# A fused RWKV-7 recurrence and expert mixture: a reciprocal and a block turn moved in VectorE's stated order, and five more filler products on TensorE

## The chip, the cores and the metric

The kernel runs on one core of a Trainium2 chip. The metric is the time of one execution on the device in microseconds (us), median of several runs. Before the change it is 1106.38 us, the median of three runs between 1105.45 and 1107.4. One further execution was taken by the profiler: it lasted 1112.95 us, and 1110.9 us of it lie between its first and its last instruction.

## The reference, cut to what matters

The inputs r, k, v, w, a, b have the shape (4, 8, 768, 40): batch, heads, tokens, width of a head. The first part walks along the tokens with a state of 40x40 for each head; the second part is a mixture of four experts with ReLU, weighted by normalized probabilities, over the 3072 rows of 320 that the first part gives.

```python
for t in range(S):
    y[:, :, t] = np.einsum('bhd,bhde->bhe', rt, state)
    Sa = np.einsum('bhde,bhe->bhd', state, at)
    state_decay = state * wt[:, :, None, :] - np.einsum('bhd,bhe->bhde', Sa, bt)
    state = state_decay + np.einsum('bhd,bhe->bhde', vt, kt)
...
x = np.ascontiguousarray(attn_out.transpose(0, 2, 1, 3)).reshape(B * S, H * D)
for e in range(E):
    h = np.maximum(x @ w1[e], 0.0)
    out += p[:, e:e + 1] * (h @ w2[e])
```

## The kernel before, in words

**Units.** The recurrence is computed in chunks of 64 tokens. A unit is one chunk for two of the four batches, with all eight heads, so that the 128 partitions hold 2 x 64 tokens (or, turned, two heads of 64 channels). There are 12 chunks and 24 units, numbered `u` = 0 to 23; units 2c and 2c+1 belong to chunk c. Names such as `M15` or `AT16` in VectorE's order mean the instruction of that kind for that unit.

**What happens for one unit.** `within` (L501) turns the decays and takes their running product (`G`, `scan`, L566), takes the reciprocal of it (`1/gp`, L582 for units from 8 on, where the decays lie by channel), turns and scales a into `AT` (L624, L626), and b and k into `NT` and `KT` (L638 to L644: the turn of k, then its product with `gp`). TensorE multiplies these into the 64x64 matrix `F` of each head (`pfe`, L663), which ScalarE copies out (L669). `substitute` (L716) inverts the unit triangular matrices of `F`: VectorE copies two parts of `blocks` (L721) and ScalarE two, VectorE turns them into `M` (L733), clears the diagonal (`M0`, L739), and folds every second column into the first by the two operations `Z1` (L745) and `Z2` (L749, whose output is `M` again). Then GpSimd runs 16 steps of one product (L763) and two sums (L780) on `Z`. `merge` (L786) turns the result on VectorE (`Qc` L791, `QTc` L792), and TensorE completes the inverse by the products `pY` and `pQ`. `step` (L824) applies the inverse to the state (`prn`, `psat`, `pxr`, `pdy`), adds up outputs and state on VectorE, and sends the output rows by DMA into `xT`, the input of the mixture.

**The mixture** of a chunk (`mixture_of_chunk`, L1070) fills TensorE's time between those products. For each expert and each half of its hidden units, `up_last` and `up_main` compute `ph` (in two PSUM buffers), ScalarE makes `hs` of it with ReLU (L976), and VectorE forms five sums of `hs` for an expert (`sum_a`, L1102: tiles a1, a7, a5, a2, a6, numbered through the kernel). The second products `p431`, `p75`, `p26` are scaled by a gate and added into `osb` on VectorE (L991), one or two operations with `gate` and one with `minus_gate` for each product. `ph` and these products share three PSUM buffers in turn (the tag `mm`).

**What sets the order.** The main loop (L1309 to L1429) calls the generators of several units piece by piece: in the turn of `u` it runs the step of `u`, the substitution of `u + 2` on GpSimd, and the loads of `u + 3`. TensorE's instructions keep this order (`stated`, L104). VectorE's order is left to a scheduler, which goes by the order of the calls and their priority, and is bound by pairs "this one ahead of that one" (L1433 to L1442): the list `VECTOR_ORDER` for the early units and lists of pairs for the later ones, among them `ahead_of_merge`. An engine runs its instructions strictly in the order of the built program, and waits where an input is not there. SyncE (SP) issues nearly all DMAs, also in order. The tile `gp` has one buffer, `rawA` (the loaded a) too; `AT` has two.

**The start.** In the first 45 us unit 0 is computed alone, and there VectorE runs the 16 steps of the substitution itself (L763, L774). TensorE has little to do; `keep_warm(n)` (L1209) gives it n products of the identity with itself, whose result nobody reads. Each counts as two matmuls in the profile. One group of ten stands at L1252, directly before `pY` of unit 0.

Of the kernel before, what the change touches and what calls it, by code (L numbers as in the profile page):

```python
# [33 lines left out]
def kernel(  # L34
# [48 lines left out]
    NU = NC * B // 2  # L83
# [25 lines left out]
    def matmul(**k):  # L109
        return stated(nc.tensor.matmul(**k))  # L110
# [101 lines left out]
    BY_CHANNEL = 8  # L212
# [53 lines left out]
    def load(q, names):  # L266
        for x in names:
            if x == "V":
                t = sb.tile([P, H, D], FP32, name="natV", tag="natV", bufs=2)[:]
            else:  # L270
                t = by_tokens(x, q.u)
            q.n[x] = t
            for i, bb in enumerate(q.b):
                nc.sync.dma_start(
                    out=t[i * L:(i + 1) * L], in_=srcs[x][bb, :, q.c * L:(q.c + 1) * L, :].rearrange("h t e -> t h e"),
                )
# [914 lines left out]
    def run(gen, n=99):  # L1191
        if gen is None:
            return
        for _ in range(n):
            if next(gen, gen) is gen:
                break
# [12 lines left out]
    def keep_warm(n):  # L1209

        for _ in range(n):
            ins = matmul(out=warm[:, 0:P], lhsT=ident[:], rhs=ident[:], start=True, stop=True)
            tc.keep_in_program_order(ins)
# [35 lines left out]
    keep_warm(8)  # L1249
    run(norm, 1)  # L1250
    run(ws[1], 1)
    keep_warm(10)  # L1252
    load(units[2], "W")
    for x in "VR":
        load_padded(units[2], x)
# [181 lines left out]
    ahead_of_merge = [(f"QTc{u - 1}", f"{x}r{u}.{i}") for u in range(BY_CHANNEL, NU) for x in "BK" for i in range(2)]  # L1437
    ahead_of_merge += [(f"QTc{u - 1}", f"RH{u - 1}.{r}") for u in range(BY_CHANNEL, NU) for r in range(2)]
    ahead_of_merge += [(f"QTc{u - 1}", f"VC{u}.{r}") for u in range(BY_CHANNEL, NU) for r in range(2)]
    in_second = [("Zr1.14", "out0"), ("out0", "Zm1.16")]  # L1440
    for one, then in [*zip(names, names[1:]), *((f"out{n}", x) for n, x in moved), ("blocks0.3", "VCv1"), ("blocks0.3", "ETc0.0"), ("blocks1.3", "Zu1.0"), ("blocks1.3", "Zu1.3"), *turned_ahead, *in_second, *waits_of_scalar, *ahead_of_merge]:
        tc.add_manual_dep(made[then].ins, made[one].ins.name, BEHIND, reason="stated order of VectorE")  # L1442
# [30 lines left out]
```

## Time and profile before

| | us |
|---|---|
| median of three runs | 1106.38 |
| the profiled execution | 1112.95 |
| its span, first to last instruction | 1110.9 |
| TensorE (PE) busy | 1071.4 (96%) |
| VectorE (DVE) busy | 808.5 (73%) |
| GpSimd (POOL) busy | 538.7 (48%) |
| ScalarE (ACT) busy | 343.9 (31%) |
| mean granted clock of TensorE | 0.977 |

A line of the timeline gives the start of an instruction (or of several alike) from the span's start, its duration, the engine, the line of the kernel, the operation with its output and inputs, and in square brackets how long the engine had been idle before it and what released it. A line of the view by stretches gives for each stretch the busy time of each engine with its count of instructions, then the clock granted to TensorE (1.00 is full speed), the share of the DMA engines that was busy and the traffic. A line of the view of waits has who waited, for whom, and then the sum of the waits in us, how many, and the longest.

### The profile page before, as it was taken

The numbers are of one execution on the slowest core, as the hardware profiler recorded it, in microseconds if no ns is written. First come the engines' busy times: TensorE is split into PE (matmuls) and PEld (weight loads), VectorE is DVE, ScalarE is ACT, GpSimd is POOL, SyncE is SP. The second block draws the span as 40 slices with busy tenths as digits, with TensorE's granted clock in tenths as the row PEclk, the third lists the DMA queues.
The fourth block names the chain that finished last, engine by engine and source line by source line (L and its number), as shares of the span: only waits on it lengthen the run. The fifth ranks groups of instructions, "written<-read, shape, count | busy, mean of one in ns | idle before, by whom it ended". The sixth has DMA issues, their size and how long they took to land.

```text
span 1110.9 us, 38458 instructions
## 1 busy us (share of the span) xinstructions
PE 1071.4 (96%) x16012; PEld 960.2 (86%) x16012; DVE 808.5 (73%) x1565; ACT 343.9 (31%) x942; POOL 538.7 (48%) x1322
## 2 busy tenths in 40 slices
PE   7899999999999999999999899899899989999998
PEld 7778888888989889899889889898898988998887
DVE  7786779996886977877959678686785967553443
ACT  3433444332322323323333323233232332321110
POOL 6116777746447356457355463553635546430000
PEclk9899999999999999999999899899999989999999
DMA  6775643435444444543453542443444343031230
GB/s 119 192 200 127 136 105 108 102 80 108 118 88 107 109 93 96 114 103 91 108 116 85 111 98 62 113 119 61 102 111 94 85 109 91 25 92 56 62 94 12
DMA packets 275349, 111.04 MB, mean 100 GB/s; under 512 B 229816, under 2 KB 254952, under 8 KB 275176
## 3 DMA queue, kind: packets, MB, share of 16 engines
q1 hardware_dynamic: 271192, 107.75, 42.1%
q8 instruction: 126, 2.06, 0.8%
q10 hardware_dynamic: 3984, 0.84, 0.4%
q14 instruction: 47, 0.39, 0.1%
HBM read 100.65 MB, written 3.93 MB: 94 GB/s over the span
## 4 chain that ended last, share of the span: by engine, by line
PE 47%; POOL 22%; DVE 17%; issue 7%; SPq 4%; DMA 2%; ACT 1%; ACTq 0%; DVEq 0%; POOLq 0%
PE ph L110 20%; PE p L110 16%; POOL Z L780 14%; POOL Z L763 8%; DVE M L733 3%; DVE a L1102 3%; SPq L936 2%; DVE osb L991 2%; SPq L302 2%; PE po L110 2%; PE pdy L110 1%; PE prn L110 1%; DVE blocks L721 1%; DVE Z L745 1%; DVE M L749 1%
## 5 line engine op out<-in xcount | busy, mean ns | idle before, releaser
L780 POOL TENSOR_TENSOR Z<-Z 128x31 f32<-128x31 f32 (+7 forms) x704 | 258.1, 367 | 55.1
L110 PE MATMUL ph<-xT,w1b 128*128 128x256 f32 (+3 forms) x1536 | 228.3, 387 | 0.5 <-issue 0.5
L110 PE MATMUL ph<-xT,w1a 128*128 128x256 f32 (+3 forms) x1536 | 225.8, 385 | 0.0
L1102 DVE TENSOR_TENSOR a<-hs 128x512 f32<-128x512 f32 x220 | 156.1, 728 | 91.5 <-ACT hs L976 91.5
L976 ACT ACTIVATE hs<-ph 128x512 f32<-128x512 f32 (+1 forms) x208 | 116.6, 565 | 311.4 <-PE ph L110 308.8
L763 POOL TENSOR_TENSOR Z<-M,Z 128x62 f32<-128x62 f32 (+7 forms) x352 | 148.0, 421 | 107.0 <-DVE M L749 81.2
L110 PEld LDWEIGHTS ph<-xT,w1b 128*128 128x128 f32 (+1 forms) x1536 | 172.5, 166 | 28.4 <-issue 7.0
L110 PEld LDWEIGHTS ph<-xT,w1a 128*128 128x128 f32 (+1 forms) x1536 | 171.1, 165 | 28.8 <-issue 7.7
L110 PE MATMUL p<-sums,a 128*128 128x160 f32 x1056 | 164.9, 299 | 0.0
L991 DVE SCALAR_TENSOR_TENSOR osb<-p,gate,osb 128x320 f32<-128x320 f32 (+1 forms) x243 | 107.6, 481 | 65.9 <-PE p L110 62.7
L110 PEld LDWEIGHTS p<-sums,a 128*128 128x128 f32 x1056 | 152.8, 190 | 2.2
L726 POOL COPY below<-F 32x256 f32<-32x256 f32 x48 | 29.3, 611 | 218.3 <-ACT F L669 153.6
L110 PEld LDWEIGHTS p<-w,hs 128*128 128x128 f32 x704 | 98.6, 190 | 9.0 <-issue 7.8
L110 PE MATMUL p<-w,hs 128*128 128x160 f32 x704 | 104.9, 302 | 0.4 <-DVE osb L991 0.4
L110 PE MATMUL p<-w,a 128*128 128x160 f32 x704 | 102.8, 299 | 0.0
L110 PEld LDWEIGHTS p<-w,a 128*128 128x128 f32 x704 | 98.0, 190 | 0.0
L798 POOL COPY QT<-QTc 32x256 f32<-32x256 f32 x96 | 44.1, 460 | 60.7 <-DVE QTc L792 54.4
L896 ACT COPY RS<-pxr 64x256 f32<-64x256 f32 x88 | 32.4, 368 | 115.6 <-DVE SX L499 80.9
L791 DVE STREAM_TRANSPOSE Qc<-Z 128x256 f32<-128x256 f32 x24 | 14.9, 621 | 57.6 <-POOL Z L780 57.4
L582 DVE RECIPROCAL gp<-G 128x512 f32<-128x512 f32 x16 | 53.6, 3352 | 0.5
L733 DVE STREAM_TRANSPOSE M<-blocks 128x1024 f32<-128x1024 f32 x24 | 47.0, 1958 | 1.7 <-ACT blocks L721 0.6
L707 ACT COPY EV<-pev 64x160 f32<-64x160 f32 x96 | 23.1, 288 | 80.1 <-PE pev L110 79.8
(167 smaller groups left out, 1458.6 us busy)
## 6 DMA issues: line engine op xcount, KB each, us to landing
w1a<-in_moe_w_dram SPq DMA_DIRECT2D x37, 512.0 KB
w1b<-in_moe_w_dram SPq DMA_DIRECT2D x37, 512.0 KB
w<-in_moe_w_dram SPq DMA_DIRECT2D x4, 1280.0 KB
w1a<-in_moe_w_dram SPq DMA_DIRECT2D x74, 64.0 KB
w1b<-in_moe_w_dram SPq DMA_DIRECT2D x74, 64.0 KB
out_dram<-osb SPq DMA_DIRECT2D x45, 80.0 KB
rawW<-in_w_dram SPq DMA_DIRECT2D x48, 72.0 KB
natV<-in_v_dram SPq DMA_DIRECT2D x42, 80.0 KB
```

The source lines that it names most:

```text
L110: return stated(nc.tensor.matmul(**k))
L582: pin(noted(nc.vector.reciprocal(out=gp[:], in_=G[:, :, 1:L + 1]), "1/gp", q.u))
L707: nc.scalar.copy(out=of_slot(q.EV[half(p)], i ^ p)[:, :, 0:D], in_=pev[i][half(p)])
L726: tc.keep_in_program_order(nc.gpsimd.tensor_copy(out=q.below[quarter(i)], in_=q.F[quarter(i), :, 0:Q]))
L733: ins = nc.vector.transpose(out=M[:], in_=cols)
L763: ins = eng.tensor_tensor(out=Z[:, 1:3, 0:n, j + 1:Q], in0=M[:, j:j + 2, None, j + 1:Q].to_broadcast([P, 2, n, m]), in1=Z[:, here, 0:n, j: ...
L780: eng.tensor_tensor(out=z[:, 0], in0=z[:, 0], in1=z[:, x], op=ALU.add)
L798: ins = nc.gpsimd.tensor_copy(out=q.QT[quarter(i), :, quarter(i % 2)], in_=QTc[quarter(i)])
L896: nc.scalar.copy(out=RS[half(s), x ^ s::2], in_=prs[x][half(s)].rearrange("p (j i) t -> p j i t", i=2),)
L976: ins = nc.scalar.activation(out=h[:, i * HF // 2:(i + 1) * HF // 2, 0:n], in_=ph[i][:], func=ACTF.Relu,)
L991: ins = nc.vector.scalar_tensor_tensor(out=to, in0=p, scalar=sc, in1=to, op0=ALU.mult, op1=ALU.add)
L1102: ins = nc.vector.tensor_tensor(out=t[:], in0=x, in1=y, op=op)
```

## The change

The call before the first `pY` gets 15 instead of ten fillers, and two lists of pairs join the stated order of VectorE. The first asks that the reciprocal of unit u+2 go ahead of five A sums of the mixture; the second that `M` of unit u go ahead of the turn of `AT` of unit u+1.

```diff
@@ -1249,7 +1249,7 @@
     keep_warm(8)
     run(norm, 1)
     run(ws[1], 1)
-    keep_warm(10)
+    keep_warm(15)
     load(units[2], "W")
@@ -1437,6 +1437,8 @@
     ahead_of_merge += [(f"QTc{u - 1}", f"VC{u}.{r}") for u in range(BY_CHANNEL, NU) for r in range(2)]
+    ahead_of_merge += [(f"1/gp{u + 2}", f"sum_a{10 * u - 45 + n}") for u in range(BY_CHANNEL, NU - 2) for n in range(5)]
+    ahead_of_merge += [(f"M{u}", f"AT{u + 1}") for u in range(BY_CHANNEL, NU - 1)]
     in_second = [("Zr1.14", "out0"), ("out0", "Zm1.16")]
```

Set side by side, the two built programs differ in these places and no others. On TensorE five fillers more stand before the first `pY`. On VectorE the turn of `AT` and its product with `G` move in three places (units 9, 10 and 11), and the reciprocal in four (units 16, 18, 20 and 22); in the other places of the two lists the stated order held already. On SP one piece of `rawA` (32x8x48 elements) of the start is issued in front of four pieces of weights instead of behind them. The orders of VectorE, before on the left:

```
AT (units 9 and 10, from the AT turn on)   | 1/gp (units 16, 18, 20, 22), from the scan on
before              after                  | before                      after
turn AT             gate, sum_a, minus     | scan                        scan
gate, sum_a, minus  blocks (2)             | a1, KT turn (2)             KT turn (2), KT x gp
blocks (2)          M                      | a7, KT x gp                 1/gp
AT x G              turn AT                | gate p75, a5, minus p75     gate p75, gate p26
M, M0               M0, AT x G             | gate p26, a2, minus p26     minus p75, minus p26
Z1, Z2              Z1, Z2                 | a6                          a1, a7, a5, a2, a6
                                           | blocks (2), 1/gp, M         blocks (2), M
```

For unit 11 the turn of `AT` stood before far ahead of `M10`, between the two operations on `NT`, and its product with `G` behind the scan; after the change both stand between `M10` and `Z1` as in the other two places.

## The prediction

> **What bounds the kernel now.** The page first: PE is busy for 96% of the span. That is an average, so the next view is the one of waits: what does TensorE still wait for?
>
> ```profile
> PEld pY L110 <- issue: 24.5, 17, 2.9
> PE pY L110 <- DVE QTc L792: 24.2, 14, 2.8
> ```
>
> Nearly all of its waiting stands before one product, `pY`, and ends with the turn `QTc` of VectorE. The timeline of PE tells where:
>
> ```profile
> 12.02 0.63 PE L113 MATMUL pNT<-ident,n_tok 128*128 128x128 f32 x4 [1.32 <-DVE n_tok L618]
> ...
> 31.80 0.68 PE L110 MATMUL pY<-QTc,below 64*64 64x64 f32 x16 [2.38 <-DVE QTc L792]
> ...
> 318.86 0.59 PE L110 MATMUL pY<-QTc,below 64*64 64x64 f32 x13 [1.04 <-DVE QTc L792]
> ...
> 574.27 0.59 PE L110 MATMUL pY<-QTc,below 64*64 64x64 f32 x13 [1.53 <-DVE QTc L792]
> ...
> 620.48 0.98 PE L110 MATMUL pY<-QTc,below 64*64 64x64 f32 x13 [2.82 <-DVE QTc L792]
> ```
>
> From 574 on the gaps alternate: 1.52 to 1.53 at 574, 667, 759, 851 and 943, and 2.78 to 2.82 at 620, 713, 805 and 897 (call them the short and the long gaps). A gap costs more than itself, as the view by stretches shows around the two (PEclk is the third number from the right):
>
> ```profile
> 574.00:576.00 2.00, 1.73 (x82) 1.76 (x86) 0.79 (x3) 0.96 (x4) 1.58 (x4) 0.82 0.17 49
> 576.00:578.00 2.00, 2.00 (x30) 1.69 (x26) 1.65 (x6) 0.71 (x3) 0.00 (x0) 0.50 0.15 31
> 578.00:580.00 2.00, 2.00 (x22) 1.75 (x20) 1.96 (x3) 1.03 (x4) 0.00 (x0) 0.82 0.61 117
> ```
>
> The short gap is followed by half speed for (0.18 + 0.50 + 0.18) x 2 / 0.5 = 3.4 us, the long one by 6.8 (same sum over 618 to 628). The gaps of 1.32 and 1.04 in the timeline above are not: their stretches read 1.00. In work: from the start of `pY` to the start of the `p` product behind the next 128-row `ph` it takes 6.43 us at 276, where the gap is 0.30 (282.46 - 276.03), 8.05 at 574 (582.32), 9.36 at 620 (629.84). So a short gap costs 1.53 + 1.62, a long one 2.82 + 2.93.
>
> What makes a long gap long? VectorE ahead of it:
>
> ```profile
> 578.73 1.23 DVE L566 TENSOR_TENSOR_SCAN G<-G,first 128x520 f32<-128x520 f32 x1
> 583.15 0.69 DVE L1102 TENSOR_TENSOR a<-hs 128x512 f32<-128x512 f32 x1 [3.19 <-ACT hs L976]
> 583.76 0.77 DVE L324 STREAM_TRANSPOSE KT<-rawK 128x256 f32<-128x256 f32 x2
> ...
> 589.08 1.43 DVE L721 COPY blocks<-F 32x256 f32<-32x256 f32 x2
> 590.54 3.35 DVE L582 RECIPROCAL gp<-G 128x512 f32<-128x512 f32 x1
> 593.81 1.88 DVE L733 STREAM_TRANSPOSE M<-blocks 128x1024 f32<-128x1024 f32 x1
> ...
> 619.24 0.61 DVE L791 STREAM_TRANSPOSE Qc<-Z 128x256 f32<-128x256 f32 x1 [4.46 <-POOL Z L780]
> ```
>
> `blocks` is done, and `M` waits behind a reciprocal that only unit 16 needs, a turn later. From `M` the chain of waits goes without slack through `Z1`, `Z2`, GpSimd's 16 steps, `Qc` and `QTc` to `pY`. And VectorE stood idle 3.19 us earlier, behind the scan that the reciprocal reads.
>
> **The reciprocal (four places, each before a long gap).** New order: the scan ends at 579.96; the two turns of k (0.69), its product (0.60), the reciprocal (3.30): 584.6. `KT` needs `rawK`, whose four DMAs SP issues from 565.07 to 567.65, 12.3 us ahead; in the turn before 367.85 they were issued until 357.74, and `KT` ran 10.1 us later without waiting, so I expect no wait. `p75` is ready about then (PE runs its 16 passes from 582.32, done about 584.65): first gate 0.46, 585.1. The second gate waits for `p26`, done on PE about 586.9, and now all five A sums stand behind it. Then: gate 0.46, two minus 0.30 each, five sums 0.61 each, `blocks` 1.45, together 5.6: `M` at 592.5 instead of 593.81. Of the 3.3 us that the reciprocal takes out, 1.3 reach `M`; the rest becomes idle time before the second gate. Bounds: if nothing were lost there, 2.8 (the whole gap); if `KT` waited for `rawK` until 583.7, -0.6.
>
> A side cost: the next `ph` (587.28) takes the PSUM buffer of `p75`, free after its minus: 587.06 before, about 587.7 now. PE stands about 0.45 us there, but the remaining gap at `pY` covers it: 2.82 - 1.3 = 1.5 splits into 0.45 there and 1.05 before `pY`. Without that cover it would cost 4 x 0.45 = 1.8 in all. The sums' readers are late enough: `a1` is read about 595, made by 589.
>
> The clock: a gap of 1.05, or even 1.3, is of the kind that no half speed followed. So a long gap loses 1.3 + 2.93 = 4.2 us, four of them 16.9. What is late next is the short gap; its `M` is paced by the gates behind PE's products (632.05 and 634.23 both wait for PE) and moves along with PE, so its 1.52 stay. Its half speed may not: today the turns repeat every 92.2 us, and every short gap is punished alike; half speed comes in portions of 3.4 us, and 92.2 is 27 of them. With a turn of about 88 the gaps drift against these portions, and one that straddles a border has less than 1.32 us on either side. I count one of the five, 1.6; bounds 0 and 8.1.
>
> Here the Trainium skill speaks against the gain. "TensorE: Matmul & The Clock Gate", section "Why this matters for your kernels", asks only that gaps stay under about 3 us. By it neither the gap of 2.82 nor that of 2.38 would be punished, and the sum would be 4 x 1.3 = 5.2. The rows above have half speed after 1.53 us, and I go by them.
>
> **`M` ahead of the turn of `AT` (three places).** The turn (0.63) and its product with `G` (0.61) leave the place before `M`, but come back between `M` and `Z1`; GpSimd's first step waits for `Z2`:
>
> ```profile
> POOL Z L763 <- DVE M L749: 81.2, 22, 6.0
> ```
>
> For units 9 and 10 the sum up to `Z2` is the same: 0, at most -0.1 each for the 0.08 us between `M` and `M0` that the turn now fills. For unit 11 both come from far ahead (363.50 and 367.24). That costs nothing only while VectorE is dense from there to `M10` at 379.09, and it stays so: the gates would start 1.24 earlier, at 371.4 and 373.9, with `p75` and `p26` done on PE about 371.0 and 373.3. If they waited all the same: up to 1.24, which makes a gap of 1.02 into 2.3, with its half speed up to 4 us. I take 0. `rawA` is free later; SP's next loads into it stand at 318.88, 338.87 and 382.74, the turns will end about 295.3, 338.4 and 380.7: no wait.
>
> **Five fillers.** Ten take 2.40 us at 27.02, so five take 1.2, inside the gap of 2.38 before `pY` of unit 0, which waits for `QTc` (31.30, VectorE's own substitution, untouched). The gap becomes 1.18, below 1.32. Half speed from 32.6 to 39.4 would go. On the chain in it stand `pg` 0.85, `pQ` 1.05, `psat` 1.77, `pst` 0.82, `pxr` 0.92: 5.4, half of it 2.7; but ScalarE's copies between `pY`, `pQ` and `pxr` take their time, and `SX` (39.44) can't start before VectorE's reciprocal ends at 36.96. I take 1.9; bounds 0 (half speed stays) and 2.5. TensorE is dense from 45 to 107, so it is not given back. SP's moved piece falls into a stretch where SP stood waiting (40.07 to 42.73): 0.
>
> **Sum.** -16.9 - 1.6 - 1.9 = -20.4, against the profiled execution 1112.95 - 20.4 = 1092.5. The median of the unprofiled runs lies 6.6 below that execution; no view tells why, so I carry the difference over: 1106.38 - 20.4 = 1086.
>
> **Rivals.**
> - *The gap shrinks, half speed stays.* The limit lies somewhere between 1.32 and 1.53, by few gaps; a long gap's `pY` and `prn` are light work around it. Then a long gap becomes a short one: 1.3 + (2.93 - 1.62) = 2.6, four times 10.4, and nothing at the start: 1096.
> - *Nothing arrives.* VectorE's work between the scan and `M` is the same in sum; if `KT` can start only at 583.1, `M` (10.7 us behind it in the new order) stands at 593.8 as before. With the fillers' 0 to 1.9: 1105.
> - *Slower: `KT` at the head of the queue waits for its load.* Before, `a1` stood ahead of it and covered the wait until 583.15; now `rawK` landing after 583.1 holds the reciprocal, the gates and `M`. The chain of waits does name a DMA just before `KT`, ending 583.72. Then `M` is 0.6 late, the gap 3.4, and a third portion of half speed adds 1.3: four times 1.9, 7.6, less what the fillers bring: 1112. Against it: the 10.1 us above.
>
> **Chances.** Forecast (long gaps lose their half speed) 0.60; half speed stays in part 0.24; nothing arrives 0.08; slower 0.08. The forecast's own range is 1079 (all five short gaps freed as well) to 1091. The range reaches from 1079 to 1100, so that the second case is in and the last two, 0.16, are out. Differences under 0.2% (2.2 us) can't be told from none here: faster 0.84, same 0.08, slower 0.08.
>
> **What would show it.** The reciprocals of units 16, 18, 20 and 22 directly behind `KT`, started about 1.4 us behind the scan's end; an idle time of about 1.8 us before the gate of `p26`; `M` 12.5 us behind the scan's end instead of 13.9; gaps before `pY` near 1.05 at 32, 620, 713, 805 and 897, with 1.00 behind them; the turn down from 92.2 to 87 or 88; `Z2` of units 8 to 10 where it was. Wrong it would be if `KT` or the first gate shows a wait for a DMA, if PEclk still falls behind gaps near 1 us, or if the saved time turns up as a longer short gap.

## The result, and the profile after

| | before | after |
|---|---|---|
| median of the runs beside each other (us) | 1106.89 (1105.45 to 1109.43) | 1095.13 (1094.94 to 1097.85) |
| the profiled execution | 1112.95 | 1094.94 |
| its span | 1110.9 | 1092.8 |
| mean granted clock of TensorE | 0.977 | 0.995 |

The ratio of after to before is 0.9897, with a 95% interval from 0.9873 to 0.9921. The forecast was 1086, the range 1079 to 1100. The kernel became faster, by 11.8 us instead of 20.4.

The view of waits of the changed kernel, the same two lines as before:

```profile
PEld pY L110 <- issue: 21.5, 17, 2.2
PE pY L110 <- DVE QTc L792: 19.8, 14, 2.1
```

The waits for `QTc` fell only from 24.2 to 19.8 us. The timeline of TensorE tells which gaps are left:

```profile
402.58 0.59 PE L110 MATMUL pY<-QTc,below 64*64 64x64 f32 x13 [1.61 <-DVE QTc L792]
571.32 0.59 PE L110 MATMUL pY<-QTc,below 64*64 64x64 f32 x13 [1.51 <-DVE QTc L792]
615.74 0.80 PE L110 MATMUL pY<-QTc,below 64*64 64x64 f32 x13 [2.12 <-DVE QTc L792]
794.13 0.59 PE L110 MATMUL pY<-QTc,below 64*64 64x64 f32 x13 [2.08 <-DVE QTc L792]
```

The short gaps stayed at 1.5, as forecast, and the one at 31.77 is 1.09 (1.18 was forecast). The long ones went from 2.8 to 2.1, where 1.05 was forecast. At 402.58 a gap grew from 1.02 to 1.61. What changed most is what follows a gap. In the profile before there are 15 portions of half speed (3.41 us each), two at the start and 13 behind 570; after, three are left, at 615.95, 704.70 and 882.19, all behind long gaps. None stands behind a short gap or at the start.

VectorE at the place of the change, in the timeline after (scan of unit 16 to `M15`):

```profile
575.41 1.23 DVE L566 TENSOR_TENSOR_SCAN G<-G,first 128x520 f32<-128x520 f32 x1
...
582.30 0.55 DVE L991 SCALAR_TENSOR_TENSOR osb<-p,gate,osb 128x320 f32<-128x320 f32 x1 [0.51 <-PE p L110]
...
583.35 4.83 DVE L1102 TENSOR_TENSOR a<-hs 128x512 f32<-128x512 f32 x5
588.10 0.77 DVE L721 COPY blocks<-F 32x256 f32<-32x256 f32 x2
588.98 1.98 DVE L733 STREAM_TRANSPOSE M<-blocks 128x1024 f32<-128x1024 f32 x1
```

The order is the forecast one: `KT` (576.56) waited for no load, and the reciprocal runs from 578.07. `M` starts 12.34 us behind the scan's end (12.5 was forecast), but on another way: the idle time before the gate of `p26` is 0.51 instead of 1.8, and the five sums take 0.97 each instead of 0.61. GpSimd in the same stretch shows what stands beside them:

```profile
583.64 1.45 POOL L726 COPY below<-F 32x256 f32<-32x256 f32 x2 [10.61 <-ACT F L669]
585.17 1.19 POOL L729 TENSOR_TENSOR n_tok<-n_tok,decay 128x320 f32<-128x320 f32 x1
586.31 1.32 POOL L729 TENSOR_TENSOR k_tok<-k_tok,decay 128x320 f32<-128x320 f32 x1
```

In the order before, these two products stood elsewhere:

```profile
589.50 0.87 POOL L729 TENSOR_TENSOR n_tok<-n_tok,decay 128x320 f32<-128x320 f32 x1
590.32 0.92 POOL L729 TENSOR_TENSOR k_tok<-k_tok,decay 128x320 f32<-128x320 f32 x1
```

The first ran beside the copies of `blocks` (589.08 to 590.51), the second beside the reciprocal. So there are two questions. Where does the gain come from, the shorter gap or the clock? And what takes back the rest of the reciprocal's 3.3 us?

### The profile page after: what moved, and what is told of

It is laid out like the page before. It is cut to its first block, busy times and chain, and to the rows that moved or that the text cites. A ratio compares the mean times of both kernels' runs of the same rounds, so it can differ in the third digit from the quotient of the medians.

```text
span 1092.8 us, 38476 instructions
## 1 busy us (share of the span) xinstructions
PE 1057.6 (97%) x16022; PEld 947.0 (87%) x16022; DVE 812.2 (74%) x1565; ACT 343.3 (31%) x942; POOL 543.6 (50%) x1322
## 4 chain that ended last, share of the span: by engine, by line
PE 49%; POOL 27%; DVE 14%; issue 6%; SPq 2%; DMA 1%; ACT 1%; DVEq 0%; POOLq 0%; ACTq 0%
PE ph L110 21%; PE p L110 17%; POOL Z L780 17%; POOL Z L763 10%; DVE a L1102 3%; DVE M L733 3%; PE prn L110 2%; PE po L110 2%; DVE blocks L721 1%; DVE osb L991 1%; PE pdy L110 1%; DVE M L749 1%; DVE Z L745 1%; PE pY L110 1%; DVE Qc L791 1%
## 5 line engine op out<-in xcount | busy, mean ns | idle before, releaser
L110 PE MATMUL ph<-xT,w1b 128*128 128x256 f32 (+3 forms) x1536 | 225.1, 377 | 0.5 <-issue 0.5
L110 PE MATMUL ph<-xT,w1a 128*128 128x256 f32 (+3 forms) x1536 | 222.7, 375 | 0.0
L1102 DVE TENSOR_TENSOR a<-hs 128x512 f32<-128x512 f32 x220 | 159.6, 749 | 78.2 <-ACT hs L976 78.2
L110 PEld LDWEIGHTS ph<-xT,w1b 128*128 128x128 f32 (+1 forms) x1536 | 170.3, 163 | 28.8 <-issue 7.0
```

What stands on the lines that cost most here:

```text
L1102: ins = nc.vector.tensor_tensor(out=t[:], in0=x, in1=y, op=op)
```

## The experiments

My theory after the result: nearly all of the gain is clock, won because the gaps fell otherwise into the portions of half speed; at equal clock the moved reciprocal brings little, since the sums now stand beside GpSimd's products and slow down. The rival: the shorter chain to `M` is itself the gain.

### The kernel before, once more (e1_before)

No edit.

> The kernel before, unchanged, to see whether its profiled execution (1112.95 us, every gap before pY from 574 on followed by half speed: 3.4 us after the short ones, 6.8 after the long ones) was typical of its runs (median 1106.9). If half speed depends on where a gap falls against a grid of 3.41 us that runs free of the kernel, executions differ: this one has 1105 to 1113 us, the gaps are again 1.5 and 2.8, but fewer of them are followed by half speed (by the clock: 6.6 us less than the profiled execution are about four portions of 1.3 to 1.6). If instead profiling itself costs the 6.6 us, this profile lies again at 1113 with the same nine punished gaps.

Measured: 1103.19 median (1100.94 to 1111.73), beside 1105.62 (1100.59 to 1113.17, 29 runs) of the same kernel; ratio 0.998 [0.9952, 1.0008]. Its profiled execution took 1103.96, with the same gaps (1.53 and 2.77) and 8 portions of half speed behind 570 instead of 13. So one kernel, with the same gaps, draws more or fewer of them from run to run, and the execution that the prediction started from, 1112.95, was among the longest. So the 6.6 us above the median are not what being profiled costs. A smaller cost is not ruled out: of the 13 other profiled executions of this study eight lie above the median of their kernel, by up to 4.4 us, and four below it, by at most 0.4.

### The parts of the change alone (e2_fillers, e3_recip, e4_m)

Each is the kernel before with one part:

```diff
-    keep_warm(10)
+    keep_warm(15)
```
```diff
+    ahead_of_merge += [(f"1/gp{u + 2}", f"sum_a{10 * u - 45 + n}") for u in range(BY_CHANNEL, NU - 2) for n in range(5)]
```
```diff
+    ahead_of_merge += [(f"M{u}", f"AT{u + 1}") for u in range(BY_CHANNEL, NU - 1)]
```

> The five fillers alone. Theory: the gap before the first pY shrinks from 2.38 to about 1.1, the 6.8 us of half speed behind it go, pY of unit 8 (276.03 before) comes 1.9 us earlier, and the end too: about -1.9. Rival: half speed behind that gap was bad luck of one execution, and the time is within 0.5 of the kernel before.

> The reciprocal ahead of the A sums alone. Theory: everything from 574 on that the profile after showed comes from it: long gaps 2.1 instead of 2.8, a turn of two units of about 89 instead of 92.2 us; of the 11.8 us between the medians some 8 to 9. In the four places the five A sums take 0.9 to 1.0 each and M stands 12.3 us behind the scan's end. Rival: the order alone does little and the fillers' shift against the clock's grid made the difference: under 4.

> M ahead of the turn of AT alone (units 8 to 10). My prediction says 0. The profile after had pY of unit 11 1.0 us earlier than the fillers' 1.9 explain (2.9 at 445), so the theory now is -1.0, gained at units 8 and 9 where the product with G (0.6 to 1.2 us) no longer stands beside GpSimd's products, less a gap of 1.6 instead of 1.0 at unit 10. Rival: 0, and the 1.0 came from elsewhere.

Measured: fillers alone 1106.72, ratio 1.000 [0.9977, 1.0023]; the reciprocal alone 1095.95, ratio 0.9912 [0.988, 0.9944]; `M` alone 1105.08, ratio 1.0002 [0.998, 1.0024]. All that can be measured of the change comes from four moved reciprocals (9.7 us, where 8 to 9 were expected). The intervals of e2 and e4 are some 2.5 us wide to either side, so neither run decides between its theory (-1.9 and -1.0) and 0. The traces say more about the fillers. In ten of the 14 profiles, with ten fillers or with 15, TensorE falls to half speed already between 22 and 25 us, so ahead of the gap, which is then 1.06 at most. In the other four the gap is there, and the fillers did what was forecast: with ten (before and e11) it is 2.4, with half speed behind it; with 15 (after and e9) it is 1.1 to 1.3, with none.

### TensorE kept at full speed, in both orders (e6_gap_fillers, e8_before_gap_fillers)

Five identity products stand in front of `pY` of units 14 to 22, in `pY`'s own bank, which `pY` overwrites. In e6 the changed kernel has them, in e8 the kernel before, with its order of VectorE in the four places pinned.

```diff
             p = (of_mixture if q.u == 0 and name == "pY" else big)(name)
+            for _ in range(FILL if name == "pY" and q.u >= 14 and q.u < 23 else 0):
+                matmul(out=p[:, 0:P], lhsT=ident[:], rhs=ident[:], start=True, stop=True)
```

> The changed kernel, with five products of the identity in front of pY in units 14 to 22, into pY's own PSUM buffer (overwritten by pY), 1.2 us in gaps of 2.1 and 1.5. They add work and take no wait away. Theory (what is left of the gaps' cost above their length is half speed, and TensorE's idle time decides it): no half speed after 570, three portions of about 1.5 saved: 1090 to 1091, and runs within 1 of each other. Rival (light work or the kernel's phase decides, not idle time): 1095, or later if the fillers delay pY.

> The kernel before with the same five products in front of pY in units 14 to 22, and VectorE's order of before stated for the four places, since the scheduler would else move the reciprocals too. Theory (at equal clock the moved reciprocal brings next to nothing: from pY of unit 14 to pY of unit 16 it is 89.49 us in the second profile of before and 89.35 after, with one portion of half speed in each; its whole gain is half speed that a gap of 2.1 draws less of than one of 2.8): with fillers the gaps here draw none either, the 8 to 13 portions of 1.5 go, and the time is that of e6_gap_fillers within 1, about 1091. Rival (the 1.3 us by which M was to come earlier count): 4 x 1.3, some 5 us, above e6_gap_fillers.

Measured: e6 1091.99, ratio 0.9871 [0.9834, 0.9908]; e8 1092.43, ratio 0.9872 [0.9835, 0.9909]. Behind 570 neither shows any half speed. Without half speed the two orders are within 0.5 us of each other, less than their runs spread (1091.63 to 1094.12, and 1091.66 to 1093.47). The timelines give the moved reciprocal 0.1 us a place (below). The rival falls. And some 14 us of the kernel before (by the ratio) are half speed behind these gaps.

### What slows the sums: GpSimd's order (e5_decay_first)

The changed kernel, with the two products of L729 issued ahead of the copies of `below` instead of behind them; they need nothing of these copies.

```diff
-        for i in (1, 3):
-            tc.keep_in_program_order(nc.gpsimd.tensor_copy(out=q.below[quarter(i)], in_=q.F[quarter(i), :, 0:Q]))
         if q.u >= BY_CHANNEL:
             for x in (q.N, q.K):
...
+        for i in (1, 3):
+            tc.keep_in_program_order(nc.gpsimd.tensor_copy(out=q.below[quarter(i)], in_=q.F[quarter(i), :, 0:Q]))
```

> The changed kernel, with GpSimd's two products by the decay (L729, about 2 us together) put ahead of its copies of F instead of behind them, so that they run while GpSimd waits for F and not beside VectorE's A sums and blocks. In the profile after, the five A sums take 4.83 us beside these products (0.6 each elsewhere), and M stands there in spite of the freed reciprocal. Theory (the two engines slow each other when they run at once): the sums go back to about 3.1 to 3.5, M comes 1.3 to 1.7 earlier in the four places and some tenths to 1.5 in the other units from 8 on, long gaps fall from 2.1 to about 0.6, short ones below 1, and no half speed is left: 1095 minus 4 x 1.5, minus some 3 of the short gaps, minus three portions of 1.5: about 1081. Rival (five sums in a row are slow by themselves, or the products only move their toll to the turns behind QTc): the time stays within 3 of 1095.

Measured: 1081.35 (1080.45 to 1083.67), ratio 0.9769 [0.9729, 0.981]. GpSimd's timeline at the place:

```profile
574.68 0.87 POOL L727 TENSOR_TENSOR n_tok<-n_tok,decay 128x320 f32<-128x320 f32 x1
575.51 0.87 POOL L727 TENSOR_TENSOR k_tok<-k_tok,decay 128x320 f32<-128x320 f32 x1
```

and VectorE's:

```profile
584.92 3.69 DVE L1102 TENSOR_TENSOR a<-hs 128x512 f32<-128x512 f32 x5
```

The products run while GpSimd would wait for ScalarE anyway; the sums take 0.74 each, `M` starts 11.0 behind the scan's end instead of 12.34, the gaps at 404 and from 570 on are 0.7 to 0.8, and no half speed follows one. The time and the step of `M` are what the theory expected; the sums stayed above its 3.1 to 3.5, as the copies of `below` still stand beside them.

### GpSimd's order without the change (e11_before_decay_first)

The same exchange in the kernel before.

> The kernel before with nothing but GpSimd's two decay products ahead of the `below` copies. Theory (in the four long places these products stood beside the reciprocal and the copies of blocks, which they do not slow, so moving them brings nothing there; in the short places it takes the gap from 1.5 to 0.7): long gaps stay at 2.7 with one or two portions of half speed each, short gaps lose theirs; 1094 to 1100. Rival (GpSimd's order alone is worth the 14 us that it brought on top of the change, whatever VectorE's order): 1082 to 1092.

Measured: 1088.31, ratio 0.9847 [0.9822, 0.9872], on the rival's side and 6 us better than the end of my theory. My error was about the long places: I had taken the copies of `blocks` for untouched. In e1 (the kernel before) they were not:

```profile
585.78 1.43 DVE L721 COPY blocks<-F 32x256 f32<-32x256 f32 x2
```

With the products early (e11):

```profile
584.86 0.68 DVE L721 COPY blocks<-F 32x256 f32<-32x256 f32 x2
```

So the long gaps went from 2.77 to 1.98, and the short ones from 1.53 to 0.68, without half speed behind them. This exchange on GpSimd alone does more (18 us) than the change (12 us). And from e11 to e5 the change is worth 7 us (8 to 9 by the ratios): with the products out of the way of its sums, the long turns become 0.7 shorter each, and the last three portions of half speed (e11 has them at 615.89, 704.64 and 878.72) go.

### The wait for p26 (e7_minus_first, e10_minus_alone, e12_minus_pinned)

In the changed kernel the minus of `p75` stands behind the gate of `p26`, and so `p75`'s PSUM buffer comes free late. Three tries to move it, four times each, in the changed kernel:

```diff
+    ahead_of_merge += [(f"out{16 * u - 67}", f"out{16 * u - 66}") for u in range(14, NU - 2, 2)]
```

is e7. e10 adds a pair that puts the first sum behind the minus of `p26`, and e12 puts all five there:

```diff
+    ahead_of_merge += [(f"out{16 * u - 65}", f"sum_a{10 * u - 45 + n}") for u in range(14, NU - 2, 2) for n in range(5)]
```

> The changed kernel, with the minus of p75 ahead of the gate of p26 in the four places, so that the PSUM buffer that the next ph waits for comes free about 0.5 earlier. My prediction says that this wait is covered by the gap before pY: theory: the ph waits no more, the long gap grows from 2.1 to about 2.5, the time stays at 1095 within 1 (above it if the longer gap brings a second portion of half speed, up to 1101). Rival (the wait is on the path): 4 x 0.45 less, 1093.

> The changed kernel in which only the minus of p75 goes ahead of the gate of p26 in the four places; the five sums stay behind the minus of p26. Theory (the free PSUM buffer is worth little, since TensorE's 0.5 us for it was covered by the gap; the gain of the run before it came from the sums that went into the wait): the stall before the next ph goes, the gap before pY grows from 2.1 to about 2.5, half speed as in the changed kernel; 1094 to 1096, up to 1101 if the longer gap draws a second portion of half speed. Rival (the wait for the PSUM buffer is on the path, and the minus brought the gain): 1082 to 1093.

> The changed kernel in which only the minus of p75 changes places with the gate of p26, four times; all five sums stay behind the minus of p26. Theory (the gain of the two runs before came from the sums that went into the wait for p26, so that GpSimd's products no longer stood beside them): the sums start 0.3 earlier and still take 0.97 each, the 0.5 us stall before the next ph goes, and the gap before pY stays at 2.1 to 2.4 with half speed behind most of them; 1093 to 1096. Rival (the PSUM buffer of p75 freed early is what brought the 12 us): M about 10 us behind the scan's end, long gaps under 0.5, 1082 to 1084.

Measured: e7 1082.0, ratio 0.9784 [0.9746, 0.9822], a miss for both theories; e10 1083.07, ratio 0.9794 [0.9766, 0.9821], on the rival's side; e12 1095.11, ratio 0.9906 [0.9871, 0.994]. The built orders tell why. Neither e7 nor e10 was the edit that I meant: with the minus ahead of the gate, VectorE's scheduler also put two of the sums into the wait (gate p75, a sum, minus, gate p26, a sum, minus, three sums); in e10 the pair held back one sum, and another took its place. Only in e12 do nothing but the minus and the gate change places. TensorE's stall before the next `ph` then goes, and the gap takes over what the stall had covered. e12 in the timeline of TensorE:

```profile
618.31 0.59 PE L110 MATMUL pY<-QTc,below 64*64 64x64 f32 x13 [2.48 <-DVE QTc L792]
```

and of VectorE:

```profile
585.93 4.83 DVE L1102 TENSOR_TENSOR a<-hs 128x512 f32<-128x512 f32 x5
```

So e12 came out as its theory had it: the buffer freed early is worth nothing here, and the 12 us of e7 and e10 come from the sums that start earlier. VectorE's and GpSimd's timelines in e7 show the other side of it:

```profile
585.09 1.88 DVE L1102 TENSOR_TENSOR a<-hs 128x512 f32<-128x512 f32 x3
584.78 2.66 POOL L726 COPY below<-F 32x256 f32<-32x256 f32 x2 [10.61 <-ACT F L669]
```

Now it is GpSimd that is slow (two copies 2.66 instead of 1.2), while the last three sums take 0.63 each. The products come from 587.52 on, when VectorE goes on to `M` (587.69). `M` starts 9.9 behind the scan's end.

### Both together (e9_both)

The exchange of e5 and the pairs of e7.

> The changed kernel with both edits that gave most so far: GpSimd's two decay products ahead of the `below` copies, and the first minus ahead of the second gate with the five sums free to start in the wait for p26. Theory (what is lost at the long gaps is VectorE's sums beside GpSimd's products, and the two edits take away different parts of it: the first the slow sums, the second the wait for p26 behind which they stood): long gaps near 0, short gaps 0.7, no half speed behind 570; 1081.4 less four times 0.75, so about 1078. Rival (both edits take away the same overlap, or a next chain ends just behind this one): 1081 to 1082, with gaps as in the first of the two alone.

Measured: 1078.33 (1078.15 to 1079.45), ratio 0.9756 [0.9731, 0.9781], the time that the theory had; the best version of this study. The mean clock of the profiled execution is 1.000. The long gaps did not go to nearly 0, as expected, but short and long ones behind 500 are alike, 0.65 to 0.67 (one is 0.17). The runs lie within 1.3 us, those of the kernel before (beside e9) within 7.7: with the half speed the spread went too.

## Why the prediction was right in its direction, and wrong in its size

**The clock as the main gain: right.** It was forecast that most of the gain (four times 2.93 of 4.2) is half speed that no longer follows. e6 and e8 show more: at equal clock the reorder brings 0.5 us in all, the clock nearly everything.

**The starting point: wrong, and the larger half of the miss.** The measured 1095.13 lies outside the forecast's own range (1079 to 1091), near the 1096 of the first rival. The sum was to end at 1092.5 in the profiled execution; it ended at 1094.94, 2.4 later. The other 6.6 of the 9.1 us come from the step "no view tells why, so I carry the difference over". The profiled execution had 13 portions of half speed behind 570, the one of e1 had 8. A change that removes the half speed removes the luck as well, so it gains less from the median than from an unlucky execution. After the change both agree (1094.94 and 1095.13). And that the sum missed the profiled execution by 2.4 us only is partly luck: it was to lose 11 of the 15 portions of half speed and lost 12, but other ones, three fewer at the long gaps and four more at the short ones than counted.

**`M` 1.3 earlier: the place right, the gain wrong.** `M` was forecast 12.5 behind the scan's end and stands at 12.34. But the 13.9 of before, from which the 1.3 were counted, contained half speed. The first sum behind the scan, in e1, where no half speed follows the short gap ahead of it:

```profile
579.86 0.69 DVE L1102 TENSOR_TENSOR a<-hs 128x512 f32<-128x512 f32 x1 [1.93 <-ACT hs L976]
```

The idle time that the reciprocal was to fill is 1.93 here and 3.19 in the profile that I read: TensorE at half speed had brought the mixture's products, and with them sums and gates, later. The times from one `pY` (unit 14) to the next, from the timelines:

| us behind `pY` of unit 14 | profile before | e1 (before) | after | e12 | e11 | e5 | e9 |
|---|---|---|---|---|---|---|---|
| scan's end | 5.69 | 5.32 | 5.32 | 5.33 | 5.34 | 5.33 | 5.33 |
| `M` starts | 19.54 | 17.92 | 17.66 | 17.50 | 17.01 | 16.33 | 15.59 |
| TensorE done, `pc` ends | 43.39 | 41.77 | 42.29 | 41.77 | 41.77 | 42.30 | 41.84 |
| next `pY` | 46.21 | 44.54 | 44.42 | 44.25 | 43.75 | 43.08 | 42.50 |

From e1 to after `M` gains 0.26, and 0.12 of it reach `pY`. The same 0.12 lie between e8 (44.56) and e6 (44.44); four of them are 0.5, the difference of their medians. So the term "1.3 reach `M`" measures 0.26 at equal clock. Two errors are in it. The starting value was stretched, as said. And "five sums 0.61 each" took 4.83 us instead of 3.05, beside GpSimd's copies and products, while the copies of `blocks`, free of them now, went from 1.43 to 0.77; without the products (e5) `M` comes 1.6 earlier than in e1. I had looked for what the reciprocal could collide with on SP and TensorE, and not for what it kept off VectorE.

**The gap of 1.05: wrong.** Of the 2.77 of e1, 0.12 went to an earlier `pY` and 0.52 to TensorE's stall before `ph` (0.45 was forecast); the rest is the 2.12 of the profile after. The stall shows in the time from `pfe` to the next 128-row `ph`. In e1 it is 2.46:

```profile
583.47 0.69 PE L110 MATMUL pfe<-NT,AT 40*64 40x64 f32 x32
585.93 3.72 PE L110 MATMUL ph<-xT,w1b 128*128 128x256 f32 x16
```

After the change it is 2.98:

```profile
582.19 0.69 PE L110 MATMUL pfe<-NT,AT 40*64 40x64 f32 x32
585.17 3.72 PE L110 MATMUL ph<-xT,w1b 128*128 128x256 f32 x16
```

The gap got shorter mostly because TensorE now waits elsewhere. e12, without the stall, has 2.48 again.

**Half speed behind the long gaps: half right.** One portion stayed in three of four places instead of none. That is near the first rival (1096), which let a long gap become a short one with its half speed; but it left the short gaps their half speed and took the 1.3 for granted, so that its time agrees is in part luck.

**Half speed behind the short gaps: too small in size, and the mechanism explains part of it.** "One that straddles a border" was the mechanism; I counted one of five, all five lost it in the profiled execution. By the borders of the last section, only three of the five are cut by one (at 660.67, 749.75 and 926.68, the last with 1.41 on one side). Those at 571.32 and 837.40 lie whole in one portion and drew nothing either.

**Fillers and `M`: nothing that can be measured.** The gap that the fillers were to shorten stands in four of the 14 profiles only (in two of them shortened), so the 1.9 us belong to an execution like the one read and hardly move the median. For `AT`, the end of `Z2` behind `pY` moved from 20.20 to 19.64 at unit 8 and from 20.40 to 19.18 at unit 9, instead of staying. At unit 10 it moved from 20.35 to 20.56, and the gap there (402.58) went from 1.02 to 1.61. But e1, unchanged, has 19.58 and a gap of 0.23 at that place, so these differ between executions too. From 276 to 571 the profile after gains 1.0 on the one before (`pY` 1.90 earlier, then 2.95), of which e1 without any change has 0.8 (297.47 us for this stretch against 298.24); in e4 alone, 1.0002, this can't be told from nothing.

**The slower rival and "nothing arrives": refuted.** `KT` stood in front of the queue and did not wait. Of an earlier `M`, though, little more than nothing arrived (0.26).

## What to carry to other kernels

When an instruction is moved on one engine, ask also what it was hiding on another: here a reciprocal had stood beside one of GpSimd's products and was not slowed; the sums that took its place were, by 1.8 us in all, while the copies behind them got 0.7 back. Time lost behind a gap came in whole portions and changed from run to run here, so take the starting point from the median of many runs, count the half speed in the one execution that is profiled, and force full speed with fillers to see what an order is worth by itself. And look at the built order of an experiment before believing its name: a pair of priorities moved more than the one instruction in two of three tries.

## What the runs showed of the hardware

**Half speed goes by windows of 3.413 us, and follows those with little work.** In each profile the starts of all half-speed stretches lie whole multiples of 3.413 us apart (within 0.01 us), and they last one or two of them. So the grid can be laid over the whole execution. Two long gaps of the changed kernel, cut by the grid in two ways (views by stretches, a stretch for each window; the first number is its length, then PE's busy time; PEclk third from the right). At 615.74:

```profile
612.54:615.95 3.41, 1.29 (x44) 1.01 (x43) 1.42 (x4) 0.92 (x2) 1.68 (x8) 1.00 0.38 68
615.95:619.36 3.41, 3.41 (x94) 3.35 (x91) 2.52 (x8) 1.54 (x6) 1.78 (x4) 0.50 0.16 43
```

At 794.13, in the same kernel:

```profile
790.03:793.44 3.41, 2.02 (x41) 1.56 (x39) 0.55 (x1) 0.92 (x2) 2.20 (x9) 1.00 0.56 96
793.44:796.85 3.41, 2.72 (x111) 2.66 (x112) 3.34 (x11) 1.59 (x6) 2.02 (x4) 1.00 0.17 44
796.85:800.26 3.41, 3.41 (x23) 2.98 (x19) 3.31 (x6) 1.71 (x6) 0.00 (x0) 1.00 0.29 87
```

The gap of 2.1 that lies in one window is followed by half speed in the next; the one that a border cuts into 1.4 and 0.7 is not. But idle time alone is not it. The short gap of the kernel before, in the profile that the prediction used:

```profile
571.89:575.30 3.41, 1.88 (x92) 1.62 (x93) 1.73 (x4) 1.04 (x4) 1.80 (x7) 1.00 0.12 30
575.30:578.71 3.41, 3.41 (x69) 3.04 (x61) 2.36 (x7) 1.38 (x5) 0.65 (x2) 0.50 0.29 62
```

and in e1:

```profile
569.75:573.16 3.41, 1.88 (x64) 1.53 (x65) 1.72 (x4) 0.92 (x2) 1.70 (x8) 1.00 0.32 59
573.16:576.57 3.41, 3.41 (x106) 3.15 (x99) 2.25 (x7) 2.63 (x10) 1.06 (x3) 1.00 0.19 50
```

Both windows have 1.53 idle, and only one was followed by half speed. They differ in what else ran in them: products on 64x64 of the array, or on 128x128. I counted for each window the matmuls that start in it as (rows x columns of the array / 128²) x streamed columns; a dense window reaches some 4200. Of the windows between 60 and 1050 us that were at full speed themselves, in the 13 profiles that have a grid, 37 have under 1140, and all 37 were followed by half speed; 20 have 1140 to 1350, and 10 were; 3640 have more, and none was. The two bounds were chosen by these windows themselves, and between them neither number decides: 1344 of work with 1.73 idle was followed by half speed (after, 701.28), 1344 with 1.89 idle was not (e12, 616.42). The two windows above have 1040 and 1188. A window with 1.67 idle and 1600 of work (e6, at 402.16) went unpunished. So a limit of idle time "somewhere between 1.32 and 1.53" was the wrong measure. That the work is the cause is an inference from many windows; e6 and e8 added work but took idle time away at once, and no run changes one without the other.

The Trainium skill, "TensorE: Matmul & The Clock Gate", section "What's actually happening", states a free-running window of 3413 ns, and the grid agrees with it. The rule that the prediction weighed, gaps under about 3 us, does not hold here: gaps of 1.5 us drew half speed.

**VectorE and GpSimd slow each other, and which one pays differs.** Sums of two SBUF operands took 0.61 alone and 0.97 on average beside GpSimd's copies and products: in the changed kernel the two engines' instructions go in turn, and a sum beside a product lasts 1.35. The copies of `blocks` took 0.68 and 1.43. In e7 the delay fell on GpSimd, 2.66 for 1.2: its second copy lasts 2.21, while three sums go by at full pace. No run isolates what decides between the two. The reciprocal took 3.35 whether one of GpSimd's products ran beside it (before) or not (after). "SBUF — State Buffer", section "SBUF: two separate sides", states that the two engines share one pair of ports as an exclusive lock, taken by whichever starts first, and that VectorE needs it for instructions with two SBUF inputs or in a two-port mode. The sums (two inputs) and the reciprocal (one) agree with that, but the long wait in e7 is more than one instruction's. The copies of `blocks` have one input and were slowed too; no run here shows whether they run in such a mode.
